# Low parts of split weights summed by TensorE in PSUM, halved scratch exchange for the gates, and a reordered first batch in an mLSTM and gated-MLP kernel

## The chip, the cores and the metric

The kernel runs on one core of a Trainium2 chip. The metric is the device time of one execution in microseconds, from three runs of the kernel before (379.46 to 380.43, median 380.21). The profile is of one further execution.

## What is computed

```
h_t = C_t q_t / max(|n_t q_t|, 1),  C_t = f C_{t-1} + i v k^T      (4 batches, 8 heads, 768 steps, width 40)
x = sigmoid(o_gate) * h                                            [4, 768, 320]
h = relu(x @ w_in);  u, v = halves of h (512 each);  v_n = (v - mean) / sqrt(var + 1e-6)
v_s = w_spatial @ v_n + b_spatial;  out = (u * v_s) @ w_out        [4, 768, 320]
```

The gates f and i are stabilised by a running maximum over the steps. w_in and w_out arrive as 64-bit floats, w_spatial as 32-bit floats. Products in the second half run in the one-pass 32-bit format (fp32r), with operands split in a high and a low part, and the products high by high, high by low and low by high are added.

## The kernel before

**Attention.** The 24 blocks n of 128 steps (6 per batch, two chunks of 64 steps each) go through a pipeline. `pe_pack(n)` (L468) issues TensorE's work of a step of it: the exponents of block n+2 (`ex`, L346, into a PSUM bank), the state products of block n+1 (`DX`, L361), the products inside the chunks of n (`DX`, L369), the scores of n+2 (`SX`, L352) and the products of n with the carried state (`SX`, L378). `weights` (ACT, L383) takes the exponential, `ktw` (GpSimd, POOL, L388) multiplies it onto the keys, `decay` (POOL, L404) scales the state and `step` (VectorE, DVE, L412 and L414) adds to it, `rows` (DVE, L422 and L425) reads the finished products of block n, `keys` (L396) the scores of n+2, `norm` (L431 to L436) divides, `gated` (POOL, L442 and L443) applies the output gate, and `turn` (TensorE, L454) transposes the rows into the operand of the second half, split by `turn_h` (ACT) and `turn_l` (DVE, L466). SX and DX are one pair of banks each, so TensorE's next pack waits for `rows` and `keys`. The exponent matmul takes rows of `GM` and `AT`; the gate sums g and a are exchanged through DRAM scratch (`scr_g`, `scr_a`) and loaded for each block by `load_g` and for each half batch by `load_a` (the first batch's `AT` by `load_a_near` from SBUF).

**Second half.** `a_v` (L502) makes the v half of a block, `ln1`, `ln2` and `ln3` (ACT, DVE and POOL, L510 to L531) normalise and split it, `b_pu` (L540) makes u, `b_pb` (L548 to L550) the product with w_spatial, `b_g1` and `b_g2` (L557 to L566) gate and split it, `c_out` (L574 to L576) makes the output.

**Weights.** `cvt` turns a 64-bit weight tile into 32 bits and a rest: `field` (ACT, L211), `bit` (two DVE operations, L214 and L215, then ACT casts to the high part, L217), `bit2` (two DVE operations, L220 and L221, which make the rest, and a subtraction of the high part from the value, L228, on POOL or DVE), `end` (DVE addition of the rest, L232). w_spatial is split by a cast (ACT, L276) and a subtraction (L277, two per pack on POOL in packs 2 to 4).

**Order.** It is written by hand in one list (L597 on), and each engine runs its own instructions in that order, so an instruction that waits holds all behind it on its engine. DMAs are issued from the queues of SP, ACT and POOL. The first batch's packs 0 to 5 form a loop in which TensorE has little to do but the packs and DVE prepares the weights; then comes layer normalisation of batch 0; then a loop over eight items per batch, each with one pack of the next batch (for six items) and one of 4 x 2 tiles of u and v_s. Four PSUM banks (tag pm) rotate among ex, px, pv, pu, pb and pc.

Of the kernel before, what the change touches and what calls it, by code (L numbers as in the profile page):

```python
# [18 lines left out]
L = 64  # L19
# [15 lines left out]
def mlstm_moe(ctx: ExitStack, tc: tile.TileContext, a):  # L35
# [11 lines left out]
    ident = const.tile([128, 128], F32, name="ident")  # L47
    mask = const.tile([128, L], F32, name="mask")[0:L]
# [880 lines left out]
```

## Time and profile before

| | |
|---|---|
| median of 3 runs | 380.21 us |
| the profiled execution | 379.95 us, span 378.2 us |
| TensorE busy | 320.9 us (85%), 4426 matmuls |
| DVE busy | 226.7 us (60%) |
| ACT, POOL busy | 147.6 us (39%), 110.8 us (29%) |
| DMA | 32.48 MB, mean 86 GB/s |
| TensorE busy from 20 to 100 us | 48.3 of 80 us |
| TensorE busy from 160 to 360 us | 197.3 of 200 us |

A row of a view in order of time has the start (us from the span's start), the duration, the engine, the line of the code, the operation and its tiles; in brackets stands how long the engine had been idle and what released it. PE is TensorE's matmuls, PEld its weight loads. A group has the busy time in total, the mean duration of one in ns, and the idle time of the engine ahead of it.

### The profile page before, as it was taken

To read this page: it belongs to the slowest core of one execution; us is meant where nothing else is said; L and a number is where in the kernel's file an instruction comes from. 1 tells how busy PE (TensorE), PEld (TensorE's weight loads), DVE (VectorE), ACT (ScalarE), POOL (GpSimd) and SP (SyncE) were. 2 spreads that over 40 slices of the span, in tenths; PEclk is the share of its full clock that TensorE was granted. 3 is DMA by queue.
4 is the path that set the end of the run, shared out by engine and by line. 5 is a ranking of instruction groups with operands and counts; after the bars stand their busy time and mean duration, and the time that the engine had idled before them with its cause. 6 is when DMAs were issued, how large, how long until landed. Compare 5 with 4: busy or idle time off the path is not lost.

```text
span 378.2 us, 10587 instructions
## 1 busy us (share of the span) xinstructions
PE 320.9 (85%) x4426; PEld 293.8 (78%) x4426; DVE 226.7 (60%) x549; ACT 147.6 (39%) x335; POOL 110.8 (29%) x181
## 2 busy tenths in 40 slices
PE   1446559557398999999899999998999999999995
PEld 1245448445297889988899999888999998899994
DVE  6738989565699996245687544546874534533131
ACT  4425553545353343267332231674322217511111
POOL 5356365722364433011344230124441101100000
PEclk9999999969569999999999999999999999999999
DMA  6575753640153234100253421002400100100101
GB/s 195 167 256 154 210 171 90 202 138 27 46 183 106 91 93 148 47 2 20 71 163 119 136 89 54 1 22 70 143 3 19 36 0 1 37 17 2 52 2 52
DMA packets 16144, 32.48 MB, mean 86 GB/s; under 512 B 4040, under 2 KB 8944, under 8 KB 16096
## 3 DMA queue, kind: packets, MB, share of 16 engines
q1 hardware_dynamic: 11360, 27.25, 23.1%
q10 hardware_dynamic: 4320, 4.37, 3.3%
q8 instruction: 35, 0.57, 0.6%
q0 software_dynamic: 416, 0.18, 0.3%
q14 instruction: 13, 0.11, 0.1%
HBM read 27.22 MB, written 4.52 MB: 84 GB/s over the span
## 4 chain that ended last, share of the span: by engine, by line
PE 46%; DVE 24%; ACT 14%; issue 5%; DMA 4%; POOL 4%; SPq 1%; ACTq 1%; POOLq 0%; DVEq 0%
PE pu L540 9%; PE pb L550 7%; PE pb L548 7%; PE pb L549 7%; ACT vL L511 4%; ACT v L510 4%; DVE vL L531 3%; ACT vH L530 3%; PE pc L574 2%; PE pc L576 2%; PE pc L575 2%; DVE bits L215 2%; DMA w<-in_w_in 2%; DVE KS L396 2%; PE DX L369 2%
## 5 line engine op out<-in xcount | busy, mean ns | idle before, releaser
L548 PE MATMUL pb<-wsH,vH 128*128 128x384 f32 x192 | 67.0, 349 | 6.6 <-ACT vH L530 6.6
L550 PE MATMUL pb<-wsH,vL 128*128 128x384 f32 x192 | 65.2, 340 | 0.1
L549 PE MATMUL pb<-wsL,vH 128*128 128x384 f32 x192 | 64.9, 338 | 0.0
L559 ACT CAST big<-g 128x384 fp32r<-128x384 f32 x32 | 16.4, 514 | 74.8 <-DVE g L558 73.6
L548 PEld LDWEIGHTS pb<-wsH,vH 128*128 128x128 f32 x192 | 36.3, 189 | 7.8 <-ACT vH L530 7.7
L557 DVE TENSOR_TENSOR g<-pb,bsp 128x384 f32<-128x384 f32 x32 | 17.7, 554 | 39.3 <-PE pb L550 39.3
L518 POOL TENSOR_TENSOR st<-st,half_neg 128x1 f32<-128x1 f32 x24 | 13.2, 549 | 86.3 <-DVE st L517 86.3
L566 DVE TENSOR_TENSOR big<-g,big 128x384 fp32r<-128x384 f32 x32 | 20.0, 624 | 28.4 <-ACT big L559 28.4
L550 PEld LDWEIGHTS pb<-wsH,vL 128*128 128x128 f32 x192 | 36.2, 189 | 0.9 <-DVE vL L531 0.9
L549 PEld LDWEIGHTS pb<-wsL,vH 128*128 128x128 f32 x192 | 36.4, 190 | 0.0
L540 PE MATMUL pu<-xH,wiH 128*128 128x384 f32 x96 | 35.4, 369 | 0.0
L361 PEld LDWEIGHTS DX<-RH 64*40 64x40 f32 x704 | 11.4, 132 | 24.3 <-issue 18.7
L574 PE MATMUL pc<-woH,big 128*128 128x320 f32 x96 | 29.8, 311 | 0.5 <-ACT big L559 0.5
L576 PE MATMUL pc<-woH,big 128*128 128x320 f32 x96 | 29.7, 309 | 0.0
L575 PE MATMUL pc<-woL,big 128*128 128x320 f32 x96 | 29.6, 308 | 0.0
L361 PE MATMUL DX<-RH 64*40 64x41 f32 x704 | 14.3, 222 | 15.9 <-issue 9.8
L442 POOL TENSOR_TENSOR x<-RH,x 128x64 f32<-128x64 f32 x24 | 7.8, 327 | 66.9 <-DVE x L436 64.7
L531 DVE TENSOR_TENSOR vL<-v,vH 128x512 fp32r<-128x512 f32 x24 | 16.6, 692 | 17.7 <-ACT vH L530 17.7
L352 PE MATMUL SX<-QK 40*64 40x64 f32 x768 | 20.6, 253 | 6.8 <-DMA QK<-in_qk 6.8
L388 POOL TENSOR_TENSOR RH<-RH,W 128x320 f32<-128x320 f32 x24 | 18.0, 750 | 26.1 <-ACT W L383 22.5
L404 POOL TENSOR_TENSOR ST<-ST,DEC 104x164 f32<-104x164 f32 x40 | 19.5, 487 | 16.8 <-DVE ST L414 14.6
L454 PE MATMUL px<-ident,x 128*128 128x128 f32 x72 | 14.0, 310 | 11.2 <-POOL x L443 8.0
(345 smaller groups left out, 787.7 us busy)
## 6 DMA issues: line engine op xcount, KB each, us to landing
RH<-in_vk SPq DMA_DIRECT2D x24, 484.0 KB
QK<-in_qk SPq DMA_DIRECT2D x48, 160.0 KB
out<-ot ACTq DMA_DIRECT2D x24, 160.0 KB
big<-in_w_sp SPq DMA_DIRECT2D x6, 384.0 KB
w<-in_w_in SPq DMA_DIRECT2D x8, 256.0 KB
w<-in_w_out SPq DMA_DIRECT2D x4, 320.0 KB
w<-in_w_rem SPq DMA_DIRECT2D x2, 256.0 KB
GM<-scr_g ACTq DMA_DIRECT2D x28, 4.0 KB
```

The costliest lines, as they stand in the source:

```text
L352: nc.tensor.matmul(s_[half(e ^ hf), hf, j * L:(j + 1) * L], QK[feat(hf), e, 0, j], QK[feat(hf), e, 1, j], start=True, stop=True)
L361: nc.tensor.matmul(dc_[feat(hf), e, j * E:(j + 1) * E], rh_k(rh)[r, h], rh_v(rh)[r, h], start=True, stop=True)
L404: nc.gpsimd.tensor_tensor(out=ST[(2 * n + e + 1) % NST][0:HI], in0=state(n, e)[0:HI], in1=DEC[0:HI, 2 * k + e, b * HH:(b + 1) * HH].unsque ...
L531: nc.vector.tensor_tensor(out=vL, in0=v, in1=vH.bitcast(F32), op=ALU.subtract)
L540: nc.tensor.matmul(pu, w, x, start=i == 0, stop=i == len(terms) - 1)
L548: nc.tensor.matmul(pb, vH[:, cd], wsH[hf][:, s], start=s == 0, stop=False)
L549: nc.tensor.matmul(pb, vH[:, cd], wsL[hf][:, s], start=False, stop=False)
L550: nc.tensor.matmul(pb, vL[:, cd], wsH[hf][:, s], start=False, stop=s == NB - 1)
L566: nc.vector.tensor_tensor(out=gL, in0=g, in1=gH.bitcast(F32), op=ALU.subtract)
L574: nc.tensor.matmul(pc, gH[:, c], woH[:, d], start=d == 0, stop=False)
L575: nc.tensor.matmul(pc, gH[:, c], woL[:, d], start=False, stop=False)
L576: nc.tensor.matmul(pc, gL[:, c], woH[:, d], start=False, stop=d == 3)
```

## The change

Six things change at once.

1. **Low parts on TensorE.** For the first four tiles of w_in, the four late ones, and one half of each of four w_spatial tiles, the low part is no longer made by a subtraction and an addition: `low_pe` adds, in a PSUM bank of the tag pm, minus the high part (a one-pass matmul with a negated identity) and the value and the rest (32-bit matmuls with the identity), and ACT copies the sum into the low tile. The two remainder tiles and w_out stay as they were. In packs 2 to 4 the second half of each w_spatial tile moves from POOL to DVE.
2. **Scratch.** The gates' rows are ordered with the batch innermost, the scratch holds the exchanged halves, so that `load_g` is one DMA instead of two, and GM and AT have 84 rows instead of 88. A store to scratch is three DMAs (was one for g).
3. **Queues.** `load_g` and `load_a` are issued from POOL (were from ACT in batch 0 and from SP later), in every pack right behind `ktw`.
4. **First batch.** The loads of the blocks 1 to 3 are issued in another order, `load_a_near(1)` earlier and from SP and POOL; the second weight's bit operations move behind the first state steps.
5. **Order in a pack of the first loop.** `bit` of the next tile comes at the end of a pack, behind `norm`; `turn` and the low sums come right behind the pack on TensorE; the w_spatial split follows `bit`.
6. **Around the layer normalisation.** Pack 6 is written out between a_v of blocks 2, 3 and 4, 5; `rows` and `keys` of it come before the last two normalisations; v has 3 buffers (was 2), x 1 (was 2).

```diff
+    def store(scr, p, q):
+        m = BH // 2
+        q.dma_start(out=scr[0:m].rearrange("p u v e t -> p (u v e t)"), in_=p[0:m].rearrange("p u v x -> p (u v x)"))
         for e in range(2):
             q.dma_start(
+                out=scr[m:].rearrange("p u v e t -> p (u v) e t")[:, :, e],
+                in_=p[m:].rearrange("p u v (e t) -> p (u v) e t", e=2)[:, :, 1 - e])
...
     def load_g(n, q):
...
-        for i in range(2):
-            q.dma_start(out=g[64 + 4 * i:68 + 4 * i, 4 * i:4 * i + 4], in_=sg[4 * i:4 * i + 4].rearrange("h r t -> r h t"))
+        q.dma_start(
+            out=GM[n % 2].bitcast(F32)[64:68].rearrange("r (h t) -> r h t", h=H),
+            in_=scr_g[z, :, kk].rearrange("(h b) w e t -> b (w e) h t", b=B)[b])
...
+        def low():
+            if pe:
+                low_pe(n, his[0][1], (val, rest))
+
         def end():
             for r, lo in los:
-                nc.vector.tensor_tensor(out=lo, in0=val[r], in1=rest[r], op=ALU.add)
+                if pe:
+                    nc.scalar.copy(out=lo, in_=lows.pop(0)[:, 0:n])
+                else:
+                    nc.vector.tensor_tensor(out=lo, in0=val[r], in1=rest[r], op=ALU.add)
...
+    def low_pe(n, hi, parts):
+        pl = bank([128, 512], "pl")
+        nc.tensor.matmul(pl[:, 0:n], minus, hi, start=True, stop=False)
+        for p in parts:
+            nc.tensor.matmul(pl[:, 0:n], ident, p, start=False, stop=p is parts[-1])
+        lows.append(pl)
...
         def split(i, e_):
             hi, lo = wsH[q][:, c + i], wsL[q][:, c + i]
             nc.scalar.copy(out=hi, in_=t[:, i])
+            if e_ is nc.tensor:
+                low_pe(384, hi, (t[:, i],))
+                return lambda: nc.scalar.copy(out=lo, in_=lows.pop(0)[:, 0:384])
             e_.tensor_tensor(out=lo, in0=t[:, i], in1=hi.bitcast(F32), op=ALU.subtract)
...
     for n in range(6):
         pe_pack(n)
         weights(n + 2)
-        gates_in(n + 4, AQ)
         step(n + 1, 0)
         decay(n + 1, 1)
         ktw(n + 2)
...
+        gates_in(n + 4, PQ)
+        nxt[0]()
+        cur[2]()
         step(n + 1, 1)
         decay(n + 2, 0)
-        cur[2]()
...
+        if n:
+            turn(n - 1)
+        cur[3]()
+        if n:
+            turn_h(n - 1)
         rows(n)
         keys(n + 2)
         if n:
-            turn(n - 1)
-            turn_h(n - 1)
+            turn_l(n - 1)
         norm(n)
         gated(n)
         gate(n + 1)
...
+        cur[4]()
+        cur = nxt
+        cur[1]()
...
+        if n in (2, 3, 4):
+            w = ws0.pop(0)
+            f = w(0, T)
+            w(1, V)
+            f()
         if n == 4:
             for k in range(2):
                 a_v(0, k)
                 ln1(0, k)
...
-        if n in (2, 3, 4):
-            w = ws0.pop(0)
-            w(0, P)
-            w(1, P)
```

The order moves at three places that the prediction speaks of. In the rows below a name with a number is a buffer, and "x2" is two instructions.

On TensorE, from the transposition at the end of pack 2 to the scores of pack 3, before:

```order
L454 MATMUL px<-ident,x 128x128 x3
L346 MATMUL ex<-GM_76,AT_75 128x512
L361 MATMUL DX<-RH_101 40x41 x8
L369 MATMUL DX<-RH_100,KS_98 64x41 x16
L352 MATMUL SX<-QK_106 64x64 x16
```

and now, at the end of pack 3 and the start of pack 4 (where no tile of w_in is summed):

```order
L485 MATMUL px<-ident,x 128x128 x3
L259 MATMUL pl<-wsH_94,minus 128x384
L261 MATMUL pl<-big,ident 128x384
L377 MATMUL ex<-GM_77,AT_76 128x512
L392 MATMUL DX<-RH_102 40x41 x8
L400 MATMUL DX<-RH_101,KS_99 64x41 x16
L383 MATMUL SX<-QK_107 64x64 x16
```

The two matmuls into pl, of which the first reads the high part that ACT casts, now stand ahead of the next pack.

On ACT, the instructions of pack 2 of the first batch from the casts of the remainder tile to the next exponential, before:

```order
L217 CAST wiH<-bits 64x256 x2
L217 CAST wiL<-bits 64x256 x2
L460 ACTIVATE xH<-px 128x3x128
L392 ACTIVATE RH_103<-RH_103 128x320
L393 ACTIVATE RH_103<-RH_103,one 128x320
L211 ACTIVATE ex<-w_215 128x256
L276 CAST wsH_93<-big 128x384 x2
L383 ACTIVATE W<-ex 128x512
```

and now:

```order
L248 CAST wiL<-pl 128x256
L228 CAST wiH<-bits 64x256 x2
L228 CAST wiL<-bits 64x256 x2
L304 CAST wsH_94<-big 128x384 x2
L307 CAST wsL_95<-pl 128x384
L414 ACTIVATE W<-ex 128x512
```

The two casts of w_spatial now follow the four casts of `bit` directly and end the pack, and the copy of the sum stands ahead of the next exponential.

On POOL, in the loop over items of batch 0, around the third item, before:

```order
L388 TENSOR_TENSOR RH_102<-RH_102,W 128x320
L404 TENSOR_TENSOR ST_109<-ST_113,DEC 104x164
L404 TENSOR_TENSOR ST_110<-ST_109,DEC 104x164
L442 TENSOR_TENSOR x<-RH_100,x 128x64
L443 TENSOR_TENSOR x<-RH_100,x 128x320
```

and now:

```order
L419 TENSOR_TENSOR RH_103<-RH_103,W 128x320
L182 DMA AT_75<-scr_a 8x384 x2
L189 DMA GM_77<-scr_g 4x8x64
L435 TENSOR_TENSOR ST_110<-ST_114,DEC 104x164
L435 TENSOR_TENSOR ST_111<-ST_110,DEC 104x164
L473 TENSOR_TENSOR x<-RH_101,x 128x64
L474 TENSOR_TENSOR x<-RH_101,x 128x320
```

Three transfers are issued between the multiplication of the keys and the two decays of the state.

More of the change, by code (lines that the diff above doesn't have):

```diff
@@ L224, in bit2 @@
             for r, hi in his:
-                if r.start not in done:
+                if not pe and r.start not in done:
                     done.add(r.start)
@@ L694, in mlstm_moe @@
         gate(n + 1)
[L695 to L705 removed]
+        cur[4]()
+        cur = nxt
+        cur[1]()
+        if n == 5:
+            for k in range(2):
+                ln3(0, k)
+        if n in (2, 3, 4):
[3 more added lines that the diff above has]
+            f()
         if n == 4:
@@ L710, in mlstm_moe @@
         if n == 5:
-            for k in range(2):
-                ln3(0, k, False)
             for k in range(2, 4):
@@ L739, in mlstm_moe @@
             ws1.append(load_ws(2, 1))
+    nxt = late.pop(0) if nxt is None else nxt
+    pe_pack(6)
+    weights(8)
+    ktw(8)
+    gates_in(10, PQ)
+    cur[2]()
+    step(7, 0)
+    decay(7, 1)
+    cur[3]()
+    cur[4]()
+    nxt[0]()
     turn(5)
+    a_v(0, 4)
     turn_h(5)
+    turn_l(5)
+    step(7, 1)
+    decay(8, 0)
+    ln1(0, 4)
     ln2(0, 2)
     ln2(0, 3)
-    turn_l(5)
-    b_pu(0, 0, 0)
-    ln3(0, 2, False)
-    a_v(0, 4)
-    ln1(0, 4)
-    ln3(0, 3, False)
+    nxt[1]()
+    nxt[2]()
+    ln3(0, 2)
     a_v(0, 5)
     ln1(0, 5)
+    ln3(0, 3)
+    rows(6)
+    keys(8)
+    nxt[3]()
+    ws1[0](1, V)
+    f = ws1[0](0, T)
+    ln2(0, 4)
+    ln2(0, 5)
+    ln3(0, 4)
+    nxt[4]()
+    ln3(0, 5)
+    f()
+    norm(6)
+    gated(6)
+    gate(7)
+    b_pu(0, 0, 0)
+    b_pb(0, 0, 0)
+    cur = late.pop(0)
+    cur[0]()
     cur[1]()
     cur[2]()
-    ws1[0](0, P)
-    ws1[0](1, V)
+    load(10)
     ws1.append(load_ws(4, 1))
     wo = [load_wo(0)]
-    ln2(0, 4)
-    ln2(0, 5)
-    ln3(0, 4, False)
-    ln3(0, 5, False)
-    cur[3]()
-    cur = late.pop(0)
-    cur[0]()
-    n, prev = 6, None
+    for w in ws1[1:]:
+        w(0, P)
+        w(1, V)
+    for c in range(1, 4):
+        wo.append(load_wo(c))
+    n, prev = 7, (0, 0, 0)
     for b in range(B):
         more = b + 1 < B
-        for i in range(8):
+        for i in range(b == 0, 8):
             hf, d = divmod(i, 4)
             pack = more and i < 6
-            q = AQ if b == 0 else SP
             if pack:
@@ L821, in mlstm_moe @@
             prev = (b, hf, d)
-            if b == 0 and i == 0:
-                for w in ws1[1:]:
-                    w(0, P)
-                    w(1, V)
-                for c in range(1, 4):
-                    wo.append(load_wo(c))
             if i == (5 if b == 0 else 4):
```

212 lines of the change are left out of this document (102 added, 110 removed).

## Prediction

> **What bounds the kernel now.** I read the slices of the page first, then the views in order of time on DVE, TensorE, ACT and POOL, then the waits. Slices of the span, 9.5 us each:
>
> ```profile
> DVE  6738989565699996245687544546874534533131
> PEclk9999999969569999999999999999999999999999
> ```
>
> DVE is at 5 tenths or more in fifteen of the first sixteen slices (151 us) and lower behind, where TensorE is full (the table above has 197 of 200 us). What the change can gain or lose lies mostly in those 151 us, and shifts all that follows. The start of `rows` of the packs 0 to 5, and the first gating behind them, show the pace:
>
> ```profile
> 30.61 0.48 DVE L422 TENSOR_TENSOR xs<-SX,ET 128x328 f32<-128x328 f32 x1
> ...
> 38.01 0.49 DVE L422 TENSOR_TENSOR xs<-SX,ET 128x328 f32<-128x328 f32 x1
> ...
> 46.01 0.50 DVE L422 TENSOR_TENSOR xs<-SX,ET 128x328 f32<-128x328 f32 x1
> ...
> 55.13 0.50 DVE L422 TENSOR_TENSOR xs<-SX,ET 128x328 f32<-128x328 f32 x1
> ...
> 63.94 0.49 DVE L422 TENSOR_TENSOR xs<-SX,ET 128x328 f32<-128x328 f32 x1
> ...
> 75.06 0.49 DVE L422 TENSOR_TENSOR xs<-SX,ET 128x328 f32<-128x328 f32 x1
> ...
> 109.51 0.54 DVE L557 TENSOR_TENSOR g<-pb,bsp 128x384 f32<-128x384 f32 x1
> ```
>
> The steps are 7.40, 8.00, 9.12, 8.81 and 11.12 us, then 34.45 us of layer normalisation. Inside the third step TensorE ran its whole pack early:
>
> ```profile
> 47.14 0.79 PE L361 MATMUL DX<-RH 64*40 64x41 f32 x32 [3.40 <-issue]
> ...
> 47.68 1.11 PE L369 MATMUL DX<-RH,KS 64*64 64x41 f32 x32
> ...
> 50.42 0.90 PE L454 MATMUL px<-ident,x 128*128 128x128 f32 x3
> ```
>
> Pack 3 began at 47.14, 1.1 us behind `rows` of pack 2, and was over at 50.42, but DVE read it only at 55.13: TensorE was 4.7 us ahead. DVE's own list was the bound:
>
> ```profile
> 48.19 0.49 DVE L436 TENSOR_TENSOR x<-xs,den 128x320 f32<-128x320 f32 x1
> ...
> 48.60 0.55 DVE L466 SCALAR_TENSOR_TENSOR xL<-px,xH 128x384 fp32r<-128x384 f32 x1
> ...
> 50.40 1.12 DVE L215 SCALAR_TENSOR_TENSOR bits<-w,bits 128x256 int32<-128x256 int32 x1
> ```
> ```profile
> 49.16 1.05 POOL L443 TENSOR_TENSOR x<-RH,x 128x320 f32<-128x320 f32 x1
> ...
> 50.18 2.20 POOL L277 TENSOR_TENSOR wsL<-big,wsH 128x384 fp32r<-128x384 f32 x2
> ```
>
> L215 took 1.12 us while POOL subtracted. It is this overlap and POOL's 2.2 us ahead of `decay` that the change removes.
>
> **What it removes.** POOL's part, by group:
>
> ```profile
> L277 POOL TENSOR_TENSOR wsL<-big,wsH 128x384 fp32r<-128x384 f32 x9 | 10.2, 1149 | 0.5 <-ACT wsH L276 0.5
> L232 DVE TENSOR_TENSOR wiH<-bits,rest 64x256 fp32r<-64x256 f32 x4 | 3.7, 926 | 0.1
> ```
>
> Nine subtractions of 1.149 us leave POOL or shrink to two; DVE's additions of remainder tiles, 0.926 us each beside POOL, get nearer to 0.4. That is a gain on DVE of one to two us a pack, if DVE stays the bound. I think it does not, for this reason.
>
> **What a low sum costs, and where it stands.** No row shows an identity matmul of 256 or 384 columns. The nearest are these:
>
> ```profile
> 60.66 0.63 PE L502 MATMUL pv__894<-wiL,xH 128*128 128x512 f32 x1
> ...
> 61.09 0.63 PE L502 MATMUL pv__894<-wiH,xL 128*128 128x512 f32 x1
> ...
> 65.10 0.52 PE L361 MATMUL DX<-RH 64*40 64x41 f32 x32
> ...
> 65.44 0.65 PE L369 MATMUL DX<-RH,KS 64*64 64x41 f32 x32
> ...
> 79.30 0.90 PE L454 MATMUL px<-ident,x 128*128 128x128 f32 x3 [6.82 <-POOL x L443]
> ```
>
> A one-pass matmul of 512 columns follows the next after 0.43 us, so 384 columns cost 0.32. A 32-bit product is two instructions; 32 of 41 columns, four side by side, took 0.54 (47.14 to 47.68), 0.0675 for 41 columns, so 384 columns cost 2 x 0.63. With 0.05 for the hand-over, a sum for w_spatial is 1.6 us, one for w_in (256 columns, two 32-bit products) 1.9. The same group took 0.34 at 65.10: once TensorE is fast, both halve to 0.8 and 1.0. Below, "slow" and "fast" mean these two rates. The slices call the clock 9 tenths in all of the first 75 us, where the group still took 0.54. The Trainium skill, "TensorE: Matmul & The Clock Gate", Part 1, has half rate as the state at rest, left after a busy window of some 3.4 us and taken up again after an idle one; the trace agrees in kind: behind the idle 6.82 us ahead of 79.30, the three transpositions took 0.90 us again, as at 50.42.
>
> In packs 2 to 4 the sum waits for ACT's cast of the w_spatial half, which stands behind the casts of `bit`, which wait for DVE's last operations of the pack; and TensorE's next pack stands behind the sum. What ran in parallel at 47 to 55 us becomes a chain. ACT's casts:
>
> ```profile
> 51.56 0.82 ACT L217 CAST wiH<-bits 64x256 fp32r<-64x256 f32 x2 [3.13 <-DVE bits L215]
> ...
> 52.40 0.83 ACT L217 CAST wiL<-bits 64x256 fp32r<-64x256 f32 x2
> ...
> 54.93 0.91 ACT L276 CAST wsH<-big 128x384 fp32r<-128x384 f32 x2
> ```
>
> Terms, each against its step above:
>
> 1. Pack 1 to 2: only w_in is summed, its parts are ready. TensorE: transposition 0.56, sum 1.9, ex 0.8, pack 3.28 (47.14 to 50.42) = 6.5. Against 8.00: **-1.5**.
> 2. Pack 2 to 3: `rows` to the end of x 2.67, xL 0.5, `bit` 0.7 alone and up to 1.9 beside POOL, taken as 1.3: 4.5 us. Four casts 1.65 and the first of w_spatial 0.46: 6.6. Sum 1.6: 8.2; ex and pack 4.1: 12.3. Fast from there on it would be 4.5 + 2.1 + 0.8 + 2.1 = 9.5. TensorE would be idle some 4 us; I take 11.6, nearer to slow. Against 9.12: **+2.5**. DVE waits about 2.6 us for its own half there, and behind it the next state step.
> 3. Pack 3 to 4: the same with the two remainder additions ahead (1.5 between 0.8 and 1.9), `bit` then clear of POOL, 0.7, and half the state products (0.27 less): 5.4 + 2.1 + 1.6 + 3.8 = 12.9. Against 8.81: **+4.1**. Bounds 10.2 (fast) and 13.6.
> 4. Pack 4 to 5: as before to 5.4; one cast and one of w_spatial 0.87; sum 1.6: 7.9. Then 16 matmuls of a_v, eight slow (0.43) and eight fast (0.22): 13.1. Before, they ran by 60.66, ahead of `rows`. Then ACT's two passes and DVE's `ln2`, from these rows:
>
> ```profile
> 67.38 0.72 ACT L511 ACTIVATE vL<-v,st 128x512 fp32r<-128x512 f32 x1
> ...
> 73.16 0.14 DVE L517 TENSOR_SCALAR st<-st 128x1 f32<-128x1 f32 x1
> ```
>
> The second pass took 0.72; I count 0.8 for each, 1.6. `ln2` of two blocks took 1.9 (73.16 to 75.06), the last one 0.95. Sum 15.7, with hand-overs 15.9, against 11.12: **+4.8**. Fast all the way it is 13.4; slow to the end, with POOL's overlap, 17.5.
>
> 5. Start, up to `rows` of pack 1:
>
> ```profile
> 12.82 1.42 PE L346 MATMUL ex<-GM,AT 88*128 88x512 f32 x2 [4.37 <-DMA GM<-scr_g]
> ...
> 14.08 0.63 ACTq L180 DMA_DIRECT2D GM<-scr_g  x2
> ...
> 19.76 0.77 PE L346 MATMUL ex<-GM,AT 88*128 88x512 f32 x1 [0.38 <-DMA GM<-scr_g]
> ...
> 31.97 0.77 PE L346 MATMUL ex<-GM,AT 88*128 88x512 f32 x1 [1.19 <-DMA AT<-ap]
> ```
> ```profile
> DVE bits L214 <- ACT ex L211: 6.2, 2, 3.4
> ```
>
> DVE stood 6.2 us waiting for ACT, which was held by its transfers; these leave ACT. TensorE waited 1.19 us more for AT at 31.97. Against that, the QK and RH of a whole block now go ahead of the first g load, which before was read at 12.82; the one issued at 14.08 behind such loads was read at 19.76, 5 us. I take 2.4 for the delay, between 0.5 and 3.6: **-5.0**, bounds -6.9 and -2.
>
> 6. Layer normalisation, pack 5 to the first gating: one more `bit` and `bit2` inside (1.5), `rows` and `keys` of pack 6 fill waits, but the transposition of block 5 stands behind a sum. I count **0**, bounds -3 and +3.
> 7. Items of batch 0: POOL issues transfers between L388 and `decay`.
>
> ```profile
> 119.18 0.46 POOL L404 TENSOR_TENSOR ST<-ST,DEC 104x164 f32<-104x164 f32 x1
> ```
> ```profile
> 120.37 0.32 DVE L414 TENSOR_TENSOR ST<-DX,ST 104x164 f32<-104x164 f32 x1
> ```
> ```profile
> 25.37 1.20 POOL L163 DMA_DIRECT2D AT<-ap  x2
> ```
>
> `decay` ended at 119.64, DVE needed it at 120.37: 0.73 us of cover. A transfer costs POOL 0.6. One fits; in two of five items there are three, 1.8 us, 1.07 late each. Less one addition in the first item: **+1.7**, bounds 0 and +3.
>
> 8. Batches 1 to 3. TensorE's two stalls there:
>
> ```profile
> PE DX L361 <- POOL ST L404: 2.3, 2, 1.1
> ```
>
> A third buffer for v lets ACT run ahead, its exponential comes some 3 us earlier, and the 2.3 us go: **-2.2**. One buffer for x costs nothing while the transposition of the block before ends ahead of the next write, as in this item:
>
> ```profile
> 118.41 0.52 PE L454 MATMUL px<-ident,x 128*128 128x128 f32 x3 [1.10 <-DVE g L557]
> ```
> ```profile
> 122.78 0.49 DVE L436 TENSOR_TENSOR x<-xs,den 128x320 f32<-128x320 f32 x1
> ```
>
> There are 3.9 us between them; without this cover DVE would wait by as much as TensorE is late.
>
> Sum: -1.5 + 2.5 + 4.1 + 4.8 - 5.0 + 0 + 1.7 - 2.2 = +4.4. On the profiled 379.95 that is 384.4; this execution lies inside the three runs, 0.26 below their median, which I neglect.
>
> **Rivals.**
> *TensorE stays fast (30%).* With the sums it is nearly without a gap in packs 0 and 1, and the idle times behind may be too short to slow it. For it: 4 us of idle in pack 2 is less than the 6.82 ahead of 79.30. Then the terms are -1.8 (DVE's 6.2 bounds pack 1), +0.4, +1.4, +2.3, start -6.9, normalisation -1, items +0.6, stalls -2.2: -7.2, 372.8. Against it: 6 to 7 us of idle in packs 3 and 4, as long as the one that slowed it. By the clock gate's rule in that page an idle of 4 us may or may not hold a whole window.
>
> *Transfers on POOL come late (15%).* The g load of pack 1 is issued only behind the key product of pack 0, one pack ahead of its reader, and may need the 5 us or more seen from 14.08 to 19.76. If the first packs wait for it the 5.0 of the start are lost: 389.4. It decides from a landing of about 6 us. The Trainium skill, "SBUF — State Buffer", section "SBUF: two separate sides", warns that a DMA issued from GpSimd starves while DVE holds the shared port; no row here shows how long.
>
> *Gains and losses cancel (15%).* Slow casts of `bit` meet no POOL, a_v fast from its start, 4 us less than my sum: about 380.
>
> **How the numbers follow.** My forecast, the chain in packs 2 to 4, has 40%, with its own range 381.5 to 388. A difference of 0.3% (1.1 us) is about what a measurement of this kernel can tell from none. Slower is 40 + 15 = 55%, faster 30%, the same 15%. The range takes in the fast case and most of the late one: 372 to 390.
>
> **What would show it.** Right: in the changed profile the starts of `rows` of packs 2 to 5 stand 11 to 13, 12 to 13 and 15 to 17 us apart; TensorE's first pl matmul of w_spatial waits several us for ACT's cast; DVE's w_spatial subtraction waits for ACT; `rows` of pack 1 starts at 31 to 35 us; the stalls behind POOL in batches 1 to 3 are gone. Wrong: if pack 3 to 4 takes 9 us or less, the chain is hidden or its links are shorter; if the state products cost 0.34 through the first loop, TensorE was fast; if `rows` of pack 1 is later than 36, the start was lost to transfers.

## The result, and the profile after

The changed kernel takes 410.53 us (median of 4 executions, 409.28 to 411.41) beside 379.99 for the kernel before: ratio 1.080, interval 1.077 to 1.084. The forecast was 384.4 with a range of 372 to 390, so the sign was right and the size was not: +30.5 us instead of +4.4. The profiled execution took 409.28 us, span 407.3. In e9, e11 and e12 below, one execution each lay more than 1.5% above the fastest of its kernel; the ratios leave it out, and the profile of e11 is of that execution.

Laid beside the steps of the forecast (starts of `rows`, first gatings, in us of the span):

| stretch | before | forecast | after |
|---|---|---|---|
| 5: start to `rows` of pack 1 | 38.0 | 33.0 | 37.2 |
| 1: pack 1 to 2 | 8.0 | 6.5 | 6.2 |
| 2: pack 2 to 3 | 9.1 | 11.6 | 13.7 |
| 3: pack 3 to 4 | 8.8 | 12.9 | 13.6 |
| 4: pack 4 to 5 | 11.1 | 15.9 | 19.5 |
| 6: `rows` of pack 5 to the first gating | 34.5 | 34.5 | 38.7 |
| 7: first to last gating of batch 0 | 51.6 | 53.3 | 55.2 |
| 8: last gating of batch 0 to the end | 217.1 | 214.9 | 223.2 |

The slices of the page, 10.2 us each, DVE and TensorE's granted clock:

```profile
DVE  6576674525575899624555854445677253543131
PEclk9999765597886999899988999999999999999999
```

DVE is emptier than before in the fifth to ninth slices (6, 7, 4, 5 and 2 tenths from 41 to 92 us; the kernel before has 9, 8, 9, 5 and 6 from 38 to 85). Work is not added there; it waits. The granted clock goes down to 5 tenths between 41 and 81 us. That the slices of before show 9 tenths there does not make this a change, as the products tell: the 32 of L361 in pack 3 of the kernel before took 0.54 us (47.14 to 47.68), the same 32 now 0.57 (51.96 to 52.53, below). TensorE was slow in pack 3 before as well, but then it was ahead of DVE. The starts of `rows` of the packs 0 to 5, and the first gating, in order of time on DVE:

```profile
28.59 0.48 DVE L453 TENSOR_TENSOR xs<-SX,ET 128x328 f32<-128x328 f32 x1
...
37.25 0.48 DVE L453 TENSOR_TENSOR xs<-SX,ET 128x328 f32<-128x328 f32 x1
...
43.48 0.48 DVE L453 TENSOR_TENSOR xs<-SX,ET 128x328 f32<-128x328 f32 x1
...
57.14 0.49 DVE L453 TENSOR_TENSOR xs<-SX,ET 128x328 f32<-128x328 f32 x1
...
70.76 0.50 DVE L453 TENSOR_TENSOR xs<-SX,ET 128x328 f32<-128x328 f32 x1
...
90.25 0.49 DVE L453 TENSOR_TENSOR xs<-SX,ET 128x328 f32<-128x328 f32 x1
...
128.98 0.54 DVE L585 TENSOR_TENSOR g<-pb,bsp 128x384 f32<-128x384 f32 x1
```

Pack 3, first on ACT and TensorE, then on DVE and POOL. Before, TensorE had begun this pack 1.1 us behind `rows` of pack 2 and was over 4.7 us ahead of DVE:

```profile
47.40 0.82 ACT L228 CAST wiH<-bits 64x256 fp32r<-64x256 f32 x2 [2.92 <-DVE bits L226]
48.23 0.82 ACT L228 CAST wiL<-bits 64x256 fp32r<-64x256 f32 x2
49.07 0.92 ACT L304 CAST wsH<-big 128x384 fp32r<-128x384 f32 x2
```
```profile
49.63 0.69 PE L259 MATMUL pl<-wsH,minus 128*128 128x384 f32 x1 [5.57 <-ACT wsH L304]
50.12 1.48 PE L261 MATMUL pl<-big,ident 128*128 128x384 f32 x2
50.83 1.20 PE L377 MATMUL ex<-GM,AT 84*128 84x512 f32 x1
51.96 0.79 PE L392 MATMUL DX<-RH 64*40 64x41 f32 x32
52.53 0.98 PE L400 MATMUL DX<-RH,KS 64*64 64x41 f32 x32
```
```profile
50.03 0.56 DVE L308 TENSOR_TENSOR wsL<-big,wsH 128x384 fp32r<-128x384 f32 x1 [2.66 <-ACT wsH L304]
53.66 0.33 DVE L445 TENSOR_TENSOR ST<-DX,ST 104x164 f32<-104x164 f32 x1 [3.07 <-PE DX L400]
53.90 0.28 DVE L231 TENSOR_SCALAR ex<-bits 128x256 int32<-128x256 int32 x1
54.22 1.28 DVE L232 SCALAR_TENSOR_TENSOR rest<-w,ex 128x256 f32<-128x256 uint32 x1
55.51 1.35 DVE L239 TENSOR_TENSOR bits<-bits,wiH 64x256 f32<-64x256 f32 x1
56.89 0.33 DVE L445 TENSOR_TENSOR ST<-DX,ST 104x164 f32<-104x164 f32 x1
```
```profile
54.49 0.74 POOL L419 TENSOR_TENSOR RH<-RH,W 128x320 f32<-128x320 f32 x1
55.16 0.65 POOL L189 DMA_DIRECT2D GM<-scr_g  x1
55.83 0.74 POOL L239 TENSOR_TENSOR bits<-bits,wiH 64x256 f32<-64x256 f32 x1
```

This is the chain of the forecast, link by link: `bit` over at 47.4, four casts, the cast of w_spatial, TensorE idle for 5.57 us until it, the sum in 1.2 us, the exponents at 50.83, the pack at 51.96, DVE's half 2.66 us late. What the forecast did not have stands in DVE's last rows: behind the first state step, DVE makes `bit2` of the remainder tile (L231, L232, L239: 3.0 us, two of them 1.28 and 1.35 beside POOL's product, transfer and subtraction; L232 takes 0.42 in pack 4, where it starts behind POOL's product) before the second step and `rows` at 57.14.

### The profile page after: what moved, and what is told of

Same layout as the page of the kernel before. It is cut to its first block, busy times and chain, and to the rows that moved or that the text cites. A ratio compares the mean times of both kernels' runs of the same rounds, so it can differ in the third digit from the quotient of the medians.

```text
span 407.3 us, 10668 instructions
## 1 busy us (share of the span) xinstructions
PE 339.7 (83%) x4478; PEld 306.3 (75%) x4478; DVE 223.3 (55%) x544; ACT 152.1 (37%) x348; POOL 115.6 (28%) x200
## 4 chain that ended last, share of the span: by engine, by line
PE 45%; DVE 21%; issue 11%; POOL 8%; ACT 7%; DMA 4%; SPq 1%; ACTq 0%; POOLq 0%; DVEq 0%
PE pu L568 8%; PE pb L578 6%; PE pb L576 6%; PE pb L577 6%; DVE vL L559 2%; POOL st L549 2%; ACT vH L558 2%; PE DX L400 2%; PE pc L604 2%; PE pc L602 2%; DVE KS L427 2%; PE pc L603 2%; PE DX L392 2%; DVE rest L232 1%; PE pl L261 1%
## 5 line engine op out<-in xcount | busy, mean ns | idle before, releaser
L587 ACT CAST big<-g 128x384 fp32r<-128x384 f32 x32 | 16.4, 512 | 75.1 <-DVE g L586 73.9
L568 PE MATMUL pu<-xH,wiH 128*128 128x384 f32 x96 | 36.7, 383 | 4.8 <-ACT W L414 4.5
L585 DVE TENSOR_TENSOR g<-pb,bsp 128x384 f32<-128x384 f32 x32 | 17.7, 555 | 39.7 <-PE pb L578 39.7
L594 DVE TENSOR_TENSOR big<-g,big 128x384 fp32r<-128x384 f32 x32 | 19.5, 608 | 29.4 <-ACT big L587 29.4
L445 DVE TENSOR_TENSOR ST<-DX,ST 104x164 f32<-104x164 f32 x40 | 12.9, 323 | 24.9 <-POOL ST L435 12.3
L559 DVE TENSOR_TENSOR vL<-v,vH 128x512 fp32r<-128x512 f32 x24 | 16.6, 693 | 17.8 <-ACT vH L558 17.8
L383 PE MATMUL SX<-QK 40*64 40x64 f32 x768 | 19.5, 245 | 6.6 <-DMA QK<-in_qk 6.6
L568 PEld LDWEIGHTS pu<-xH,wiH 128*128 128x128 f32 x96 | 19.4, 202 | 7.0 <-ACT W L414 4.9
L414 ACT ACTIVATE W<-ex 128x512 f32<-128x512 f32 x24 | 14.3, 594 | 26.2 <-PE ex L377 15.4
```

What stands on the lines that cost most here:

```text
L383: nc.tensor.matmul(s_[half(e ^ hf), hf, j * L:(j + 1) * L], QK[feat(hf), e, 0, j], QK[feat(hf), e, 1, j], start=True, stop=True)
L559: nc.vector.tensor_tensor(out=vL, in0=v, in1=vH.bitcast(F32), op=ALU.subtract)
L568: nc.tensor.matmul(pu, w, x, start=i == 0, stop=i == len(terms) - 1)
L594: nc.vector.tensor_tensor(out=gL, in0=g, in1=gH.bitcast(F32), op=ALU.subtract)
```

## The experiments

All times are medians beside the kernel before on the same chip; the ratio's interval stands in brackets. The columns are the stretches of the table above, each from the one profiled execution of the kernel, while the time is the median of all its executions; "item" is the first item of batch 1 (its first to its second gating), which is part of the rest.

| kernel | us | rows 1 | 1-2 | 2-3 | 3-4 | 4-5 | norm. | batch 0 | item | rest |
|---|---|---|---|---|---|---|---|---|---|---|
| before | 379.99 | 38.0 | 8.0 | 9.1 | 8.8 | 11.1 | 34.5 | 51.6 | 6.3 | 217.1 |
| after | 410.53 | 37.2 | 6.2 | 13.7 | 13.6 | 19.5 | 38.7 | 55.2 | 9.3 | 223.2 |
| e1 | 392.82 | 37.3 | 6.2 | 8.8 | 7.6 | 16.8 | 38.5 | 54.2 | 7.0 | 220.8 |
| e2 | 402.20 | 36.4 | 6.2 | 13.2 | 13.6 | 18.6 | 37.5 | 52.1 | 10.5 | 221.2 |
| e3 | 393.85 | 37.3 | 6.2 | 7.4 | 8.2 | 16.6 | 38.8 | 54.2 | 10.6 | 224.4 |
| e4 | 385.46 | 36.6 | 6.2 | 8.8 | 7.6 | 16.4 | 38.3 | 52.0 | 7.0 | 217.0 |
| e5 | 381.26 | 35.7 | 6.2 | 8.8 | 7.6 | 16.5 | 34.7 | 51.8 | 7.2 | 217.2 |
| e6 | 384.96 | 36.8 | 6.2 | 8.8 | 10.4 | 11.4 | 39.1 | 51.7 | 9.0 | 220.0 |
| e7 | 379.25 | 33.7 | 6.2 | 8.8 | 10.4 | 11.4 | 34.8 | 51.8 | 9.9 | 220.4 |
| e8 | 401.40 | 37.1 | 6.2 | 12.0 | 12.2 | 19.4 | 38.3 | 54.2 | 6.7 | 220.8 |
| e9 | 380.75 | 34.5 | 6.5 | 7.4 | 9.8 | 13.5 | 34.7 | 51.9 | 8.9 | 220.1 |
| e10 | 377.77 | 33.9 | 7.1 | 9.8 | 10.4 | 11.4 | 34.7 | 52.0 | 6.4 | 216.7 |
| e11 | 385.14 | 39.1 | 6.2 | 8.8 | 10.4 | 11.4 | 34.8 | 51.7 | 10.2 | 223.7 |
| e12 | 380.96 | 36.8 | 6.2 | 10.2 | 9.8 | 14.2 | 34.7 | 52.0 | 6.3 | 216.9 |
| e13 | 375.85 | 34.9 | 6.4 | 8.8 | 10.4 | 11.4 | 34.8 | 52.5 | 6.3 | 216.9 |
| e14 | 380.76 | 33.2 | 6.1 | 10.4 | 10.4 | 11.4 | 34.8 | 52.3 | 10.0 | 221.0 |

### e1: w_spatial of packs 2 to 4 back on POOL

```diff
-            f = w(0, T)
-            w(1, V)
-            f()
+            w(0, P)
+            w(1, P)
```

> The changed kernel, with the low parts of w_spatial of packs 2 to 4 taken back to POOL (both halves), so that TensorE has no sum between two packs there; the low sums of w_in and the transfers on POOL's queue stay. Chain theory (DVE's bit, ACT's casts, TensorE's w_spatial sum, next pack is what the three packs lost): from the start of rows of pack 2 to that of pack 5 it takes 30 to 34 us instead of 46.7, and the time falls by 12 to 16 us, to about 395 to 399. Queue theory (the loss is in transfers that POOL issues ahead of its decays): those three steps lose no more than 3 us and the time stays above 405. Clock theory (TensorE runs at half clock whatever stands between the packs): the granted clock stays at 0.5 to 0.8 from 40 to 80 us and the steps lose less than 5 us.

392.82 us, 1.0345 [1.0313, 1.0377] of before: 17.7 us off. Packs 2 to 5 take 33.2 us in place of 46.8, 13.6 less; 2.3 more are the first item of batch 1, whose length depends on something else (e11 to e14) and is no part of the chain. The chain theory holds, with 1.7 us more in all than it asked; the queue theory does not for these steps.

### e2: transfers back on ACT and SP

The g loads of the blocks 2 and 3 and the one behind the first loop go back to ACT likewise.

```diff
-        gates_in(n + 4, PQ)
+        gates_in(n + 4, AQ)
...
-            if pack:
-                gates_in(n + 4, PQ)
+            if pack and b == 0:
+                gates_in(n + 4, AQ)
...
+                if b:
+                    gates_in(n + 4, SP)
                 load(n + 4)
```

> The changed kernel, with the one g and the two a transfers per block taken back from POOL's queue to the queues and places of before (ACT in batch 0, SP ahead of the loads of a block in the later batches); the halved scratch and all else stay. Chain theory: the three steps from rows of pack 2 to pack 5 stay at 44 to 47 us; only the items of batch 0 and the loop of batch 1 gain, 4 to 8 us, so about 403 to 406. Queue theory: 12 us or more go, to 398 or below, some of them in packs 1 to 5. If the loop of batch 1 (first state step to last gating) does not get shorter by 2 us or more, POOL's issue time ahead of decay is not what slowed it.

402.20 us, 1.0572 [1.0540, 1.0604]: 8.3 us off, a little more than the chain theory gave. Packs 2 to 5 stay at 45.5, the items of batch 0 get 3.0 us shorter. The loop of batch 1 did not get shorter, its first item is even 10.5 us here. By the words of the expectation POOL's issue time would then not be what slowed it; but the item hides it: e1 and e4, which have the same first item, give the cleaner difference, 3.9 us over batches 1 to 3.

### e3: w_spatial ahead of `bit`

```diff
         cur[4]()
+        if n in (2, 3, 4):
+            w = ws0.pop(0)
+            f = w(0, T)
+            w(1, V)
+            f()
         cur = nxt
         cur[1]()
...
-        if n in (2, 3, 4):
-            w = ws0.pop(0)
-            f = w(0, T)
-            w(1, V)
-            f()
```

> The changed kernel, with one block of the first loop moved: in packs 2 to 4 the cast, the sum on TensorE and the subtraction of w_spatial stand ahead of the next w_in tile's bit instead of behind it. Same instructions on each engine. Chain theory: ACT casts w_spatial while DVE is still at the pack's end, TensorE's sum no longer waits 5 to 10 us, and the three steps from rows of pack 2 to that of pack 5 take 33 to 38 us instead of 46.7; the time falls by 8 to 13 us. If instead the sums themselves (about 1.2 us each at the slow rate) or TensorE's half clock are the loss, the three steps stay within 3 us of 46.7.

393.85 us, 1.0362 [1.0333, 1.0391]: 16.7 us off with the same instructions, and packs 2 to 5 in 32.2 us, less than with POOL (33.2). Both are more than the chain theory asked (13 us and 33). TensorE's sums of packs 2 to 4, in order of time:

```profile
44.98 0.44 PE L259 MATMUL pl<-wsH,minus 128*128 128x384 f32 x1 [0.87 <-ACT wsH L304]
...
52.93 0.69 PE L259 MATMUL pl<-wsH,minus 128*128 128x384 f32 x1 [4.09 <-ACT wsH L304]
...
61.40 0.69 PE L259 MATMUL pl<-wsH,minus 128*128 128x384 f32 x1 [2.85 <-ACT wsH L304]
```

The waits ahead of them are 0.87, 4.09 and 2.85 us, in the changed kernel 5.57, 9.85 and 5.84. So the sum on TensorE is not what costs; the place of this block behind `bit`'s casts is.

### e4: e1 and e2 together

> Both edits of the two runs before in one kernel: w_spatial of packs 2 to 4 on POOL again, and the transfers back on the queues of before. If the two losses lie at different places, the gains add within 2 us: about 388 to 394 by the chain theory with its 12 to 16 and the queues' 4 to 8. What is left above the kernel before is then the start (rows of pack 1 at 37 us instead of the forecast 33) and the layer normalisation (first gating 4.4 us later than before, counted from rows of pack 5). If the sum of gains is less than one of them alone plus 1 us, the two are the same loss seen twice.

385.46 us, 1.0136 [1.0105, 1.0167]: 25.1 us off; e1 and e2 alone gave 17.7 and 8.3, together 26.0. The two losses are separate, and the time is 2.5 us below the range expected. 5.5 us above before are left, and the table shows where: pack 4 to 5 (+5.3), which the expectation did not name, and the normalisation (+3.9), with 1.4, 1.8 and 1.3 us gained in the start and in the steps of pack 1 to 2 and pack 3 to 4.

### e5: SP's order behind the first loop (on e4)

```diff
-    load(10)
     ws1.append(load_ws(4, 1))
     wo = [load_wo(0)]
+    load(10)
```

> The kernel of e4_both (385.46 us) with one edit on SP's queue: behind the first loop, the last two blocks of w_spatial and the first tile of w_out are loaded ahead of the block loads of block 10, not behind them. Theory of the queue order: SP stands until RH's buffer is read by pack 6, so the w_spatial load lands 4.9 us late, ACT's cast of it waits, the weights of the next pack stand behind that cast and TensorE behind these; the first gating comes 4 to 5 us earlier and the time is 380 to 382. Rival: the stretch of layer normalisation is bound by DVE's own list there; then ACT waits no more but the first gating moves by less than 1.5 us and the time stays above 384.

381.26 us, 1.0032 [1.0013, 1.0051]: 4.2 us off, normalisation 34.7. The rows that show it, in the changed kernel, on SP, ACT and TensorE:

```profile
121.83 0.35 SPq L369 DMA_DIRECT2D RH<-in_vk  x1
122.28 0.66 SPq L300 DMA_DIRECT2D big<-in_w_sp  x1
```
```profile
127.06 0.93 ACT L304 CAST wsH<-big 128x384 fp32r<-128x384 f32 x2 [4.73 <-DMA big<-in_w_sp]
```
```profile
128.53 0.69 PE L568 MATMUL pu<-xH,wiH 128*128 128x384 f32 x1 [4.50 <-ACT W L414]
```

SP issues the last w_spatial load only behind block 10's RH, whose buffer pack 6 frees at 121.8, after 25.2 us of waiting; ACT's cast of it waits 4.73 us for the data, the next pack's weights stand behind that cast, TensorE waits 4.50 us for these.

### e6: the last remainder tile in pack 3 (on e4)

```diff
-        cur[2]()
+        if n != 4:
+            cur[2]()
...
-        cur[4]()
+        if n != 4:
+            cur[4]()
         cur = nxt
         cur[1]()
+        if n == 3:
+            cur[2]()
+            cur[4]()
```

> The kernel of e4_both with one edit in the first loop: the last remainder tile is finished in pack 3 (its bit2 and its last additions right behind its bit), as in the kernel before, and not in pack 4 behind rows and norm. Theory of the late tile: in e4_both the a_v products ahead of pack 5 wait 4.7 us on TensorE for that tile, then run at the slow rate; with the edit the wait is gone, pack 4 to 5 takes 11 to 13 us instead of 16.4, pack 3 to 4 takes 2 to 3 us more than 7.55, and the time falls by 2 to 4 us to about 382 to 383.5. Rival: a_v must stand where ACT and DVE let it, and pack 4 to 5 is bound by the two passes of ACT and by ln2 behind them; then pack 4 to 5 stays above 15 and the time at 385 or more.

In e4, with no sum in the way, the a_v products had waited for that tile:

```profile
64.63 0.76 PE L533 MATMUL pv__900<-wiH,xH 128*128 128x512 f32 x1 [4.74 <-DVE wiH L250]
```

Pack 4 to 5 falls from 16.4 to 11.4 as the theory of the late tile has it, pack 3 to 4 rises from 7.6 to 10.4: 2.2 us gained in these packs. The time, 384.96 us, 1.0107 [1.0059, 1.0155], hardly moves; in the profiled execution the first item of batch 1 went from 7.0 to 9.0. The four executions fall in two pairs, 383.2 and 383.8, 386.2 and 386.3, and the profile is of the slower pair, so whether that item is slow in all of them stays open. So the mechanism is shown and the time missed its expectation.

### e7: e5, e6 and the start

```diff
-    load_qk(1)
-    load_rh(1)
     load_g(0, SP)
     load_g(1, SP)
+    load_qk(1)
+    load_rh(1)
```

> The kernel of e4_both with the edits of e5 and e6 and, at the start, the first two g loads ahead of the QK and RH loads of block 1 on SP's queue, as in the kernel before. If these are what is left of the loss, gains add: 4 to 5 (SP's order), 2 to 4 (remainder), 0 to 3 (the first exponential 3.9 us earlier, of which I expect only part at rows of pack 1, since a chain of state steps, the second half's decay on POOL and two low sums lies behind it): 374 to 379, below the kernel before. If rows of pack 1 stays at 36 us or later, the start is not bound by the first g load.

379.25 us, 0.9972 [0.9955, 0.9989]. This is just above the range expected. `rows` of pack 1 starts at 33.7, 2.0 to 3.1 us ahead of e4, e5 and e6 (36.6, 35.7 and 36.8 with one and the same start), so the order of these loads did bound the start. The first item of batch 1 takes 9.9 us here, 2.9 more than in e4.

### e8: TensorE kept busy ahead of its w_spatial sums

`idle` is 26, 40 and 26 in the packs 2, 3 and 4; the results are overwritten by the sum.

```diff
+        for _ in range(idle):
+            nc.tensor.matmul(pl[:, 0:384], minus, minus.unsqueeze(1).broadcast_to([128, 3, 128]), start=True, stop=True)
         nc.tensor.matmul(pl[:, 0:n], minus, hi, start=True, stop=False)
```

> The changed kernel with work added on TensorE only: ahead of each w_spatial sum of packs 2 to 4 stand 26, 40 and 26 matmuls of 128x384 whose results are overwritten, so that TensorE is busy through most of its wait for ACT's cast; nothing else waits for them if they end ahead of the cast (4.6 to 7 us at the fast rate). Clock theory: the slow rate of sum, ex and pack behind each wait is a part of the loss; granted clock near 1.0 up to 80 us, each of the three steps 1.5 to 2.5 us shorter, a_v 1 us shorter, together 5 to 7 us off, about 404 to 406. Chain theory alone: the added work hides and gains under 1.5 us, 409 or more; or, run at the slow rate, it outlasts the wait and costs.

```profile
PEclk9999899898886999999999999999899999999999
```

401.40 us, 1.0554 [1.0527, 1.0582]: 9.1 us off, more than expected, but not for the reason given: packs 2 to 5 get 3.1 us shorter (1.6, 1.4 and 0.1), and 2.7 are the first item of batch 1, which the 92 added matmuls may shift as in e11 to e14. The rest has no cause shown; the two profiled executions are only 7.2 us apart. The half clock is a real part of the chain's price, and the smaller one: 3.1 of the 17.7 us in packs 2 to 5 that were lost.

### e9 and e10: what the sums are worth once nothing late stands ahead of them

e9 is the changed kernel with e3's order and the edits of e7 other than e1's; e10 is e7 with `early_cvt` without TensorE's sums:

```diff
-        return cvt(src, 256, his, los, EARLY, ft_.pop(i), i < 4)
+        return cvt(src, 256, his, los, EARLY, ft_.pop(i))
```

> The changed kernel with TensorE's sums of w_spatial kept but placed ahead of bit (as in e3), and the other edits of e7: transfers on the queues of before, w_spatial and w_out loads ahead of block 10's, last remainder tile finished in pack 3, first g loads ahead of block 1's loads. Chain theory: a sum on TensorE is harmless, and a gain of POOL's 1 us pieces, where nothing late stands ahead of it: packs 2 to 5 take 29 to 31 us (30.64 in e7), and the time is 377.5 to 379.5, at or below e7's 379.25. Rival: the sums cost TensorE and ACT what POOL's subtractions cost, wherever they stand: packs 2 to 5 at 32 us or more and the time at 381 or above.

> The kernel of e7_both_and_start (379.25 us) with the low parts of the first four w_in tiles taken back to POOL and DVE (subtraction 0.9 us on POOL, addition 0.4 us on DVE, as in the kernel before), so that TensorE makes no sum before pack 3. If the sums of w_in are what made pack 1 to 2 fall from 8.0 to 6.2 us, that step is back at 7.5 to 8.5 and the time 1 to 3 us longer, 380.5 to 382. Rival: those sums stand ahead of the next pack on TensorE and are on the path as well; then the steps from rows of pack 0 to that of pack 2 do not grow and the time is 379.5 or less.

e9: 380.75 us, 1.0008 [0.9985, 1.0032], packs 2 to 5 in 30.7 us as in e7 (30.6). The sums of w_spatial on TensorE neither gain nor cost in these packs then; the rival's 32 us was not reached, nor the chain theory's gain, and the time is 1.5 us above e7. e10: 377.77 us, 0.9936 [0.9913, 0.9959], below the 380.5 expected. This is the time that the rival had, but not by its reason: packs 1 to 3 are longer, by 1.9 us, though the step of pack 1 to 2 itself takes 7.1 and not the 7.5 or more expected; the time is shorter all the same, since the first item of batch 1 takes 6.4 us here. What the sums of w_in are worth shows only between kernels with a like item (e13 and e14 are below): e13 with them is 1.9 us faster than e10 without (items of 6.3 and 6.4 us), e7 with them 1.5 us faster than e14 without (9.9 and 10.0).

### e11 to e14: the first item of batch 1

Small matmuls are added on TensorE once, near 9 us, ahead of the transpositions for the decay: 140 in e11 (on e7) and e12 (on e9), 25 in e13 (on e7) and e14 (on e10). Nothing reads their results.

```diff
         pe = bank([128, 512], "pe")
+        for _ in range(idle):
+            nc.tensor.matmul(pe[0:32, 448:480], minus[:, 0:32], minus[:, 0:32], start=True, stop=True)
```

> The kernel of e7_both_and_start (379.25 us) with 140 matmuls of 32 columns added on TensorE near 9 us, where it waits for the first exponential; their results are overwritten. Reason: the first item of batch 1 takes 7.0 us in some kernels and 9 to 10.6 in others; in the slow ones TensorE stands about 1 us at a place that the profile puts down to issue, and at the half rate behind it. Count theory: the stop comes at a fixed count of TensorE's instructions (in three kernels after some 1856 and 2364 matmuls); 140 more ahead move it out of the run of small matmuls of a pack into long ones, the item takes 6.3 to 7.3 us and the time falls by 2 to 3.5 us, to 376 to 377.5. Rival: the stop belongs to the place in the program (the first item of a batch) or to other engines; then the item stays at 9 us or more and the time within 1 us of 379.25.

> The kernel of e9 with the same 140 small matmuls near 9 us. Its TensorE list has nine matmuls more than e7's ahead of batch 1, so the stop would move by the same 140. Count theory: the same gain over e9 as e11 has over e7, 2 to 3.5 us, if e9 has the slow first item of batch 1 (9 us or more), and none if it has not. Expected time 375 to 377.5, which would be below the kernel before by about 1%.

Both missed in time. e11 took 385.14 us (1.0103 [1.0062, 1.0144]); in the profiled execution the 140 matmuls held the start by 5.3 us and the item stayed slow. e12 took 380.96 (1.0017 [0.9993, 1.0041]), 2.3 us late at `rows` of pack 1, with 3.5 us more in packs 2 to 5; its item fell from 8.9 to 6.3 us, as the count theory has it. The reason why e11's shift did nothing for the item shows in the counts. Matmuls between TensorE's stops that the profile puts down to issue, by windows that end at the stops (columns: window, length, busy time and count of matmuls, clock, DMA share, GB/s), of the changed kernel and of e11:

```profile
0.00:162.10 162.10, 104.49 (x1857) 0.85 0.40 123
162.10:212.92 50.82, 47.97 (x508) 0.94 0.17 54
212.92:299.22 86.30, 83.19 (x1264) 0.98 0.26 82
```
```profile
0.00:134.27 134.27, 98.76 (x1857) 0.91 0.47 142
134.27:141.76 7.49, 6.67 (x126) 1.00 0.33 113
141.76:190.41 48.65, 45.81 (x508) 0.98 0.17 56
```

The stops stand at 1857, 2365 and 3629 in the one, at 1857, 1983 and 2491 in the other: 508 is four times 127, 1264 ten times 126.4. A shift of 140 is one period and 13. So e13 and e14 shifted by 25.

> The kernel of e7_both_and_start (379.25 us, first item of batch 1 9.88 us) with 25 matmuls of 32 columns added on TensorE near 9 us, where it waits; results overwritten. Place theory: the stop of some 1 us after about 2364 matmuls falls 25 matmuls earlier in the program, well inside the pack of that item instead of on its last products and the one behind it, as in e12 (2342 by e7's count), whose item took 6.35: the item takes 6.3 to 7.3 us and the time falls by 2.5 to 3.5 us to 375.8 to 376.8, below the kernel before by about 1%. Rival (the state of that item is chance or belongs to the change of batch): the item stays at 9 or more and the time within 1 us of 379.25. The 25 matmuls themselves cost the start 0 to 1 us.

> The kernel of e10_w_in_on_dve (377.77 us, first item of batch 1 6.38 us) with the same 25 small matmuls. It has 20 matmuls fewer than e7 ahead of batch 1, so the stop that lay 18 behind e7's place, among long products, comes 7 ahead of it, on the last small products of the pack, as in the changed kernel and in e9 (8 to 9 ahead; 9.35 and 8.86 us). Place theory: the item becomes slow, 8.9 to 10.6 us, and the time rises by 2 to 4 us to 380 to 382. Rival: it stays at 6.3 to 7.3 us and the time within 1 us of 377.77.

e13: 375.85 us, 0.9884 [0.9866, 0.9903], item 6.3. e14: 380.76 us, 1.0038 [1.0010, 1.0067], item 10.0. No execution of e13 reaches up to one of e7, and none of e14 down to one of e10. The two kernels exchanged their first items as the place theory says. The products with the carried state in that item, in e14 and in e13 (L411 there is L409 of the changed kernel):

```profile
184.10 0.61 PE L411 MATMUL SX<-ST,QK 40*64 40x41 f32 x27
186.36 0.45 PE L411 MATMUL SX<-ST,QK 40*64 40x41 f32 x5 [1.65 <-issue]
```
```profile
184.80 0.66 PE L411 MATMUL SX<-ST,QK 40*64 40x41 f32 x32
```

e14 stands 1.65 us, five products ahead of the pack's end; e13 has no stop there. What makes the item long is more than the stop. In the item of e4 and of e7 (columns as above, the clock is the fourth number):

```profile
191.85:198.84 6.99, 5.98 (x82) 1.00 0.37 121
```
```profile
182.94:192.82 9.88, 8.49 (x77) 0.65 0.41 126
```

The clock sorts all the items of the table: 1.00 where the item takes 6.3 to 7.2 us, with a stop in it (e1, e4, e5) or without, 0.81 in e6 and e9 (9.0 and 8.9), 0.65 to 0.68 in the changed kernel, e2, e3, e7, e11 and e14 (9.3 to 10.6). Why the clock falls in one and not in the other stays open: e4 and e7 stop behind the same count (2364 and 2363; in e7 the profile names ACT as what ended it), and only e7 runs at half rate there.

## Why the prediction was wrong

The likeliest case, the chain in packs 2 to 4, is what happened, and the forecast from it was 26 us too low. In the profiled executions the sum is 24.7 us short: 8.3 in step 8, 6.3 in steps 2 to 4, 4.3 in step 6, 4.2 in step 5, 1.9 in step 7, and 0.3 the other way in step 1. By its own steps:

- **Step 1** (6.5, measured 6.2) is right as a size. That the sums of w_in alone bring it is not shown: without them the step takes 7.1 in e10 and 6.1 in e14, and the step behind it 9.8 and 10.4 where e7 and e13 have 8.8, so that 1.3 to 1.9 us of the two steps together are theirs.
- **Steps 2 to 4** were sized at +11.4 together and measured +17.7. The links were right: in pack 3 the sum was over 7.4 us behind `rows` (8.2 forecast), the pack 10.9 (11.6 taken). The sum alone took 1.2 us (49.63 to 50.83) where 1.6 was counted. The step that failed is the end: the forecast let `rows` start where TensorE's pack ends. DVE's list has `bit2` between the first state step, which needs that pack, and `rows`: 3.0 us in pack 3, where `rows` starts 2.8 us behind the end of TensorE's pack. In pack 4 the 1.6 us of `bit2` are nearly covered (`rows` at 70.8, the pack over at 70.4), and the step is 0.7 over its forecast. Ahead of pack 5 the a_v products were over at 83.4 (12.6 us, 13.1 forecast), and behind them came a whole pack, `bit2` and all of `ln2`, not its last 0.95. POOL's first power there stood behind three transfers, from the views in order of time on POOL and DVE:

```profile
86.36 1.11 POOL L182 DMA_DIRECT2D AT<-scr_a  x2
87.46 0.65 POOL L189 DMA_DIRECT2D GM<-scr_g  x1
88.13 0.47 POOL L435 TENSOR_TENSOR ST<-ST,DEC 104x164 f32<-104x164 f32 x1
88.55 0.58 POOL L549 TENSOR_TENSOR st<-st,half_neg 128x1 f32<-128x1 f32 x1
```
```profile
89.16 0.15 DVE L550 TENSOR_SCALAR st<-st 128x1 f32<-128x1 f32 x1 [1.75 <-POOL st L549]
```

  e1 and e3 show that the chain carries 13.6 to 14.5 us of the 17.7; e6 shows a second cause under it in step 4, the remainder tile that is finished one pack later, which the forecast did not see.
- **Step 5** (-5.0, bounds -6.9 and -2) measured -0.8. The term that was too small is the delay of the first exponent matmul: 3.9 us where the forecast took 2.4 and bounded it at 3.6. (With 3.6 its own sum gives -3.8; the bound of -2 has no working.)

```profile
16.69 1.19 PE L377 MATMUL ex<-GM,AT 84*128 84x512 f32 x2 [3.64 <-DMA w<-in_w_in]
```

  The row names another load as what ended the wait; that the order of the loads set it is shown by e7, where this matmul starts at 13.35. DVE's 6.2 us of waiting for ACT did go, as forecast, but 3.8 us came in their place further down the same chain, and shrank to 0.5 in e7:

```profile
DVE KS L427 <- ACT W L414: 3.8, 1, 3.8
```

  e7 gives 2.0 to 3.1 us at `rows` of pack 1 for the load order; e2 gives 0.9 for the transfers on POOL, no more than the 1.1 us by which e4, e5 and e6 differ with one start. With both undone (e7), `rows` of pack 1 stood at 33.7, the forecast's 33.0 nearly, but with a delay of 0.5 us, for which the forecast's sum gives 31.1: the 7.4 us counted for the two waits were too much as well. The text's own sign for it, later than 36, came true.
- **Step 6** was counted at 0 with bounds of 3 and measured +4.3. It failed on SP's queue: the loads of block 10 had been moved ahead of the w_spatial load, and the forecast followed ACT, DVE and TensorE there but not SP. e5 gives 3.6 of it back in that stretch.
- **Step 7** (+1.7, bounds 0 and 3) measured +3.6; with the transfers off POOL it is 0.5 (e2, e4). The mechanism was right, in-order issue ahead of `decay`, the size too small.
- **Step 8** (-2.2) measured +6.1 and is wrong in sign. TensorE's two stalls behind POOL did not go but grew, from 2.3 to 3.6 us over batches 1 to 3, and DVE's waits from 4.3 to 11.1, since POOL issues transfers between the key product and `decay` in these batches too, which the forecast had priced for batch 0 alone:

```profile
DVE ST L414 <- POOL ST L404: 4.3, 5, 1.6
```
```profile
DVE ST L445 <- POOL ST L435: 11.1, 8, 2.6
PE DX L392 <- POOL ST L435: 3.6, 2, 1.8
```

  e1 against e4 prices these transfers at 3.9 us there. 2.3 more is the first item of batch 1. With both gone (e10, 216.7; e13, 216.9) the rest is within 0.5 us of before: the stalls that the third buffer of v was to remove are not a gain that any run shows.
- **The rivals.** "TensorE stays fast" was wrong: 32 state products took 0.57 us in pack 3, not 0.34. "Gains and losses cancel" is ruled out by the time. "Transfers come late" was wrong in its mechanism, which asked for a landing of 6 us; g loads from POOL landed in 2.1 to 5.3 us, median 3.2. What they cost is POOL's own time, 0.65 us each, in the middle of a state chain. The Trainium skill, "SBUF — State Buffer", section "SBUF: two separate sides", has such transfers starve while DVE holds the shared port; no run here shows that.

In the runs' spans, taken one behind the other, w_spatial's place is 17.1 (e1, with 2.3 of the first item in it), the transfers 7.2 (e4 against e1), SP's order 4.4 (e5), and what start and remainder tile lost less the first item 1.1 (e7); this goes from 407.3 to 377.5, and the kernel before has 378.2. The range missed because it was put around one case: losses that no term had or that had too small a term, each from an instruction moved past a queue or behind a wait, all went the same way. The halved scratch and the buffers of v and x have no run of their own.

## What to carry to other kernels

Where work moves to an engine that was ahead, ask what its operand now waits for and what stands behind it on that engine: the same three sums cost 17 us behind the casts of `bit`, and ahead of them (e3, e9) those packs take no longer than with POOL's subtractions. Follow every queue that a moved line is written past, the loading one too: one line moved across another on SP was worth 4 us (e5), issues of 0.65 us on POOL ahead of the state steps 7 us over the kernel (e1 and e4). Of what the change did, the sums of w_in are shown to be worth keeping (1.5 to 1.9 us); the single transfer and the new start were kept in e13 and not priced alone. e13, with these and 25 matmuls that do nothing, is 1.2% below the kernel before.

## What the runs showed that was not expected

TensorE stops for 0.8 to 2 us at fixed counts of matmuls, which lie multiples of some 127 apart, where these fall into a run of small matmuls or just behind one; around some of the stops its clock is at half. In the changed kernel the clock had fallen ahead of the stop (0.52 from 210.2 to 212.0 us, the stop begins at 211.9), behind a wait of 1.8 us for POOL, so the stop alone is not what brings it down there. The Trainium skill, "Runtime: NRT & Kernel Launch", section "Instruction fetch mechanics", has instructions fetched in blocks of 256 and calls the cost of a block's end mostly hidden; 127 matmuls with as many weight loads are 254 instructions, which fits the period, and if the stops are these fetches, they are not hidden: moving them by 25 matmuls was worth 3.4 us one way (e7 to e13) and cost 3.0 the other (e10 to e14). The trace of the changed kernel agrees: its queue of kind instruction moves 35 packets of 16 KB, some 126 matmuls apart in the mean, and one of them starts 1.4 to 1.9 us ahead of each of the three stops. Most of the packets have no stop behind them, so that the stops are fetches is inferred from period and place, and not shown.
